# A hand-made scheduler's step estimates are set to the durations of a trace (windowed attention and two MLPs, one core)

## The chip, the core and the metric

One core of a Trainium2 chip runs the whole program as one launch. TensorE (PE) multiplies, VectorE (DVE) and ScalarE (ACT) do everything elementwise, GpSimd (POOL) only sets up constants, and SyncE (SP) issues all transfers. The metric is the device time of a launch in microseconds (us), compared as medians.

## What is computed

The reference, cut to what matters (`q`, `k`, `v` are 4 x 8 x 576 x 64, so 2304 tokens of width 512; both MLPs are 512 to 2048 to 512, all in float32):

```
scores = scale * q @ k.T;  scores = where(0 <= rel < 64, scores, -1e9)     # causal window of 64
attn   = exp(scores - max);  attn = attn / (sum(attn) + 1e-9)
x      = (attn @ v), heads side by side                                     # 2304 x 512
h = x @ w_in;  x = relu(h)**2 @ w_out                                       # first MLP
h = x @ w_in;  P = a0 + a1*h + a2*h*h + a3*h*h*h                            # second MLP, with its own weights
Q = 1 + |b0|*|h| + |b1|*h*h;  out = (P / (Q + 1e-6)) @ w_out
```

## The kernel before, in words

**Arithmetic.** Each float32 matrix of an MLP is split into a high and a low part (`wih`, `wil`, `wo`, `xh`, `xl`, `g` for both parts), and a product is three matmuls: high by high, high by low, low by high. So a weight tile that comes from memory first goes through `convert` (lines 355 to 394): a load into one of three `raw` buffers, an ACT operation (L369), three DVE operations on the bits (L371, L374, L377), a rounding on ACT (L388: the high part) and a subtraction on DVE (L389: the low part).

**Tiles and stages.** Tokens go in five blocks (four of 512, one of 256), the hidden width in 16 steps `j` of 128. Layer 0 (the first MLP) works through the blocks; a step is 12 matmuls `h` (L552, into PSUM buffers `h0`, `h1`), `mid1` on ACT and DVE (L618 relu, L620 and L623 or L624 squares, L625 the low part of `g`), and 12 matmuls into the accumulators `acc0` to `acc3` (L571), one step later. While block 0 runs, its weights are converted, and while each block runs, the attention of the next is done in between: per 128 tokens transposes of `q` and `k` (L435, L448), scores (L470), softmax on DVE, ACT and DVE (`top` L485, `exp` L490, `norm` L494 to L496), transposes of the probabilities (L507) and their product with `v` (L523), with copies out of PSUM in between (L440, L456 or L457, L512, L535, L536). The first block's attention stands alone at the start. Layer 1's weights are converted during blocks 1 to 3, stored to memory and loaded again. Layer 1 (the second MLP) has the same loops with `mid2` (L664 to L686: three ACT reads of `h`, then seven DVE operations, a logarithm and an exponential on ACT, and a rounding L685), its outputs two steps behind `h`; `h` has four PSUM buffers there. `evac2` copies the accumulators out and stores them.

**What sets the order.** Nothing is written in its final order. Each step is added to a `Plan` with its possible engines and for each an estimate in nanoseconds, its reads and writes, and sometimes a due time. `Plan.run` (L90) then builds a timetable by the estimates: it always takes the item and engine that can start first (the engine free, the inputs ready and a gap of 150 to 200 passed, 2000 after a load), and among equal starts the one that is due first. A step with two engines (copies, roundings, one of the squares) goes to the one on which it starts first. The items are emitted in that order, so the estimates decide the order of rows in each engine's queue and which of two engines does a step. They decide nothing else: at run time each engine works strictly through its own queue, waiting for semaphores. SP's loads are items too, with their own estimates.

```
119    key = (start, it.due)
295    MM = {n: 0.4167 * n + 3 for n in (256, 512)}        # one matmul of the MLPs
498    plan.add({"dve": 850}, top, [ps], [t, nm])
499    plan.add({"act": 1550}, exp, [nm, t], [t, su])
```

`act(n, psum, ptr)` and `dve(n, fast, ptr)` (L133, L137) are the estimates of an elementwise operation on n columns: `psum` when it reads PSUM, `fast` for the double rate, `ptr` for operands that are one value per partition. `start` and `span` (L297 to L305), from which the due times of both MLPs follow, are made of `MM`.

## Time and profile before

| | us |
|---|---|
| median of three runs | 895.03 |
| lowest | 893.75 |
| the profiled execution, on the device | 894.46 |
| its span in the trace (first to last instruction) | 892.7 |
| TensorE busy (matmuls) | 877.6 |
| VectorE busy | 667.3 |
| ScalarE busy | 570.2 |

Times in the trace are from the span's start. An engine's busy time counts overlapping instructions once, and ends of matmuls are modelled, so a busy TensorE need not be at its peak. In the rows further down, a bracket behind an instruction gives the idle time of its engine just before it and what ended it.

### The profile page before, as it was taken

How to read it: one execution, taken by the hardware profiler on the slowest of the kernel's cores; microseconds unless marked ns; L12 is line 12 of the kernel's file. 1: busy time of each engine (PE TensorE's matmuls, PEld its weight loads, DVE VectorE, ACT ScalarE, POOL GpSimd, SP SyncE). 2: the span in 40 equal slices, each digit the busy share in tenths (PEclk: the TensorE clock that was granted, in tenths of full speed). 3: DMA queues.
4: the chain of work that ended last, by engine and by line, in shares of the span. 5: the costliest groups of instructions: out<-in, count | busy, mean ns of one | idle time of the engine just before them, and what ended most of it. 6: DMA issues, size and time to landing. Idle time of an engine off the chain costs nothing.

```text
span 892.7 us, 14126 instructions
## 1 busy us (share of the span) xinstructions
PE 877.6 (98%) x5200; PEld 730.2 (82%) x5200; DVE 667.3 (75%) x1428; ACT 570.2 (64%) x1187; POOL 3.1 (0%) x17
## 2 busy tenths in 40 slices
PE   7899999999999999999999999999999999999998
PEld 6677788888878888888899888888888888988886
DVE  6999999878587842422131799999999999999994
ACT  6886777667566653443344766676667666888764
POOL 1000000000000000000000000000000000000000
PEclk9999999999999999999999999999999999999999
DMA  9796676878878721200079920210011002100001
GB/s 219 199 242 180 194 215 209 268 234 262 257 246 246 239 64 37 94 1 1 1 284 370 355 76 1 67 75 1 1 48 47 1 1 95 48 1 24 1 0 48
DMA packets 133573, 110.50 MB, mean 124 GB/s; under 512 B 79488, under 2 KB 112256, under 8 KB 131456
## 3 DMA queue, kind: packets, MB, share of 16 engines
q1 hardware_dynamic: 133504, 109.60, 39.1%
q8 instruction: 41, 0.67, 0.3%
q14 instruction: 28, 0.23, 0.1%
HBM read 78.65 MB, written 30.93 MB: 123 GB/s over the span
## 4 chain that ended last, share of the span: by engine, by line
PE 86%; DVE 8%; DMA 3%; ACT 2%; issue 1%; SPq 0%; POOL 0%; POOLq 0%; ACTq 0%; DVEq 0%
PE h L552 29%; PE acc L573 22%; PE acc L571 18%; PE t L552 11%; DMA raw<-in_moe_w_out_dram 2%; PE t L523 2%; DVE cvr L374 1%; DMA raw<-in_moe_w_in_dram 1%; PE t L470 1%; DVE cvr L377 1%; PE t L507 1%; DVE raw L371 1%; PE t L448 1%; DVE sm L485 1%; PE t L435 0%
## 5 line engine op out<-in xcount | busy, mean ns | idle before, releaser
L571 PE MATMUL acc<-g,wo 128*128 128x512 f32 (+1 forms) x960 | 216.0, 372 | 0.2 <-DVE g L625 0.2
L571 PEld LDWEIGHTS acc<-g,wo 128*128 128x128 f32 x960 | 166.4, 189 | 31.1 <-issue 0.9
L552 PE MATMUL h<-xh,wih 128*128 128x512 f32 (+1 forms) x480 | 181.9, 379 | 1.1 <-ACT xh L535 0.6
L552 PE MATMUL h<-xh,wil 128*128 128x512 f32 (+1 forms) x480 | 177.4, 370 | 1.1 <-DVE wil L389 1.1
L552 PE MATMUL h<-xl,wih 128*128 128x512 f32 (+1 forms) x480 | 177.3, 369 | 0.3 <-DVE xl L536 0.3
L625 DVE TENSOR_TENSOR g<-cvr,g 128x512 fp32r<-128x512 f32 (+1 forms) x80 | 50.8, 635 | 103.3 <-ACT cvr L623 103.0
L618 ACT ACTIVATE cvr<-h 128x512 f32<-128x512 f32 (+1 forms) x80 | 44.2, 553 | 95.7 <-PE h L552 90.5
L552 PEld LDWEIGHTS h<-xh,wil 128*128 128x128 f32 x480 | 90.5, 189 | 18.0 <-DVE wil L389 2.4
L552 PEld LDWEIGHTS h<-xh,wih 128*128 128x128 f32 x480 | 90.5, 189 | 17.7 <-issue 1.4
L552 PEld LDWEIGHTS h<-xl,wih 128*128 128x128 f32 x480 | 90.6, 189 | 14.2 <-DVE xl L536 0.7
L573 PE MATMUL acc<-wo,cvr 128*128 128x512 f32 x384 | 93.1, 390 | 0.0
L573 PE MATMUL acc<-wo,g 128*128 128x512 f32 x384 | 93.1, 390 | 0.0
L573 PEld LDWEIGHTS acc<-wo,g 128*128 128x128 f32 x384 | 71.6, 188 | 14.5
L573 PEld LDWEIGHTS acc<-wo,cvr 128*128 128x128 f32 x384 | 71.5, 188 | 14.4
L669 DVE SCALAR_TENSOR_TENSOR kT<-kT,b,sm 128x512 f32<-128x512 f32 (+1 forms) x80 | 55.7, 696 | 16.4 <-ACT kT L664 13.6
L671 ACT ACTIVATE raw<-kT,cb 128x512 f32<-128x512 f32 (+1 forms) x80 | 54.9, 686 | 8.7 <-DVE kT L669 4.6
L552 PE MATMUL t<-xl,wih 128*128 128x512 f32 (+1 forms) x160 | 58.9, 368 | 0.0
L552 PE MATMUL t<-xh,wil 128*128 128x512 f32 (+1 forms) x160 | 58.8, 368 | 0.0
L552 PE MATMUL t<-xh,wih 128*128 128x512 f32 (+1 forms) x160 | 58.8, 368 | 0.0
L369 ACT ACTIVATE cvr<-raw 128x512 f32<-128x512 f32 x64 | 42.7, 671 | 24.2 <-DMA raw<-in_moe_w_out_dram 14.5
L682 DVE SCALAR_TENSOR_TENSOR pT<-pT,coef,raw 128x512 f32<-128x512 f32 (+1 forms) x80 | 55.6, 695 | 1.7
L673 ACT ACTIVATE raw<-raw,cb 128x512 f32<-128x512 f32 (+1 forms) x80 | 54.5, 681 | 1.8
(143 smaller groups left out, 1332.1 us busy)
## 6 DMA issues: line engine op xcount, KB each, us to landing
raw<-in_moe_w_in_dram SPq DMA_DIRECT2D x64, 256.0 KB, 3.8
raw<-in_moe_w_out_dram SPq DMA_DIRECT2D x32, 512.0 KB, 4.2
w2h_d<-raw SPq DMA_DIRECT2D x32, 256.0 KB, 2.8
w2l_d<-cvr SPq DMA_DIRECT2D x32, 256.0 KB, 3.1
ld<-in_v_dram SPq DMA_DIRECT2D x25, 256.0 KB, 3.8
out_dram<-ld SPq DMA_DIRECT2D x18, 256.0 KB, 2.0
x2h_d<-xh SPq DMA_DIRECT2D x4, 1024.0 KB, 4.4
x2l_d<-xl SPq DMA_DIRECT2D x4, 1024.0 KB, 5.7
```

Source lines behind the costliest of these rows:

```text
L369: plan.add({"act": act(DM)}, lambda e: A.activation(out=t.t, in_=raw.t.bitcast(F32)[:, :, 1], func=ACTF.Copy, scale=2.0 ** -112), [raw], [t])
L371: plan.add({"dve": dve(DM, True)}, lambda e: V.tensor_scalar(out=raw.t[:, :, 1], in0=raw.t[:, :, 1], scalar1=0x80000000, scalar2=None, op0 ...
L523: T.matmul(out=ps.t[e * 64:(e + 1) * 64, hp, gl * W:(gl + 1) * W], lhsT=vg[gl].t[:, 2 * hp + e, :], rhs=pt[gl].t[:, hp, (e ^ gl) * 64:((e ...
L552: T.matmul(out=v4(hp.t, n), lhsT=w.t[:, (c ^ 2) * 128:((c ^ 2) + 1) * 128], rhs=x.t[:, :n // 128, c, :], start=(c == 0 and z == 0), stop=( ...
L571: T.matmul(out=v4(acc[l, bi, m].t, n), lhsT=w.t[:, m, :], rhs=y.t[:, :n // 128, :], start=st, stop=en)
L573: T.matmul(out=v4(acc[l, bi, m].t, DM), lhsT=y.t[:, m, :], rhs=w.t, start=st, stop=en)
L618: plan.add({"act": act(n, True)}, lambda e: A.activation(out=r.t[:, :n], in_=hp.t[:, :n], func=ACTF.Relu), [hp], [r])
L625: plan.add({"dve": dve(n)}, lambda e: V.tensor_tensor(out=gl.t[:, :nq], in0=v4(r.t, n), in1=gh.t[:, :nq].bitcast(F32), op=ALU.subtract), [ ...
L669: plan.add({"dve": dve(n, ptr=1)}, lambda e: V.scalar_tensor_tensor(out=f(h2), in0=f(h2), scalar=b1, in1=f(ab), op0=ALU.mult, op1=ALU.add) ...
L671: plan.add({"act": act(n, ptr=1)}, lambda e: A.activation(out=f(y), in_=f(h2), func=ACTF.Ln, scale=2.0 ** -63, bias=cb[:, 0:1]), [h2], [y])
L673: plan.add({"act": act(n, ptr=1)}, lambda e: A.activation(out=f(y), in_=f(y), func=ACTF.Exp, scale=-1.0, bias=cb[:, 1:2]), [y], [y])
L682: plan.add({"dve": dve(n, ptr=1)}, lambda e: V.scalar_tensor_tensor(out=f(u), in0=f(u), scalar=coef[:, 0:1], in1=f(y), op0=ALU.subtract, o ...
```

## The change

Only numbers that `Plan` reads are changed; no operation, buffer, load or loop is touched.

```diff
 def act(n, psum=False, ptr=0):
-    return (50 if psum else 92) + 0.836 * n + 93 * ptr
+    return (150 if psum else 180) + 0.86 * n + 90 * ptr
...
 def dve(n, fast=False, ptr=0):
-    return 68 + 1.042 * n / (2 if fast else 1) + 61 * ptr
+    return 160 + 1.03 * n / (2 if fast else 1) + 63 * ptr
...
-    MM = {n: 0.4167 * n + 3 for n in (256, 512)}
+    MM = {n: 0.4167 * n + 13.6 for n in (256, 512)}
...
-        plan.add({"dve": 850}, top, [ps], [t, nm])
-        plan.add({"act": 1550}, exp, [nm, t], [t, su])
+        plan.add({"dve": 1470}, top, [ps], [t, nm])
+        plan.add({"act": 2310}, exp, [nm, t], [t, su])
```

Besides: transposes 430 to 450, the scores 900 to 1250, the product with `v` 1250 to 1280. `norm` stays at 1050, the loads keep theirs. For 512 columns `act` goes from 478 to 590 (PSUM) and from 520 to 620 (SBUF), `dve` from 602 to 687, a matmul from 216.4 to 227.0.

What stands elsewhere now, at three places. In the names, the number behind an underscore counts buffers and differs between the two programs.

**First place: ScalarE's queue at the start**, the attention of block 0. `wih11`, `wil11`, `wih10`, `wil10` here are buffers in which softmax of the first and second 128 tokens works (`nm` and `su` its maxima and sums); `qT` and `kT` are transposed inputs. Before:

```order
L456 COPY kT0_209<-t0_204 128x4x128
L440 COPY qT0_221<-h0_214 128x512
L456 COPY kT1_219<-t1_243 128x4x128
L490 ACTIVATE wih11_248,su0_268<-wih11_248,nm0_249 128x128 x4
L490 ACTIVATE wil11_262,su1_302<-wil11_262,nm1_263 128x128 x4
L440 COPY qT0_319<-acc3_314 128x512
L512 COPY wo5_351<-t1_328 128x512
L490 ACTIVATE wih10_353,su2_376<-wih10_353,nm2_354 128x128 x4
```

After:

```order
L456 COPY kT0_209<-t0_204 128x4x128
L440 COPY qT0_221<-h0_214 128x512
L456 COPY kT1_219<-t1_245 128x4x128
L440 COPY qT1_264<-h1_256 128x512
L490 ACTIVATE wih11_250,su0_277<-wih11_250,nm0_251 128x128 x4
L490 ACTIVATE wil11_266,su1_313<-wil11_266,nm1_267 128x128 x4
L490 ACTIVATE wih10_318,su2_339<-wih10_318,nm2_319 128x128 x4
L440 COPY qT0_366<-acc3_304 128x512
```

The copy of `qT1` is new in this queue (before, VectorE did it behind eight pieces of L485), and the copy of the third `qT` has moved behind a third group of exponentials.

**Second place: one step of the second MLP in its steady state**, block 1. First TensorE, where the `h` of one step ends and the outputs (L573) of the step two before follow. Before:

```order
L552 MATMUL h1_6309<-xl0_5389,wih10_5142 128x512
L552 MATMUL h1_6309<-xh0_5363,wil10_5149 128x512
L573 MATMUL acc0_5985<-wo4_1371,g_719 128x512 x3
L573 MATMUL acc1_5992<-wo4_1371,g_719 128x512 x3
L573 MATMUL acc2_6001<-wo4_1371,g_719 128x512 x3
L573 MATMUL acc3_6006<-wo4_1371,g_719 128x512 x3
L552 MATMUL t1_6351<-xh0_5363,wih11_5174 128x512
```

After:

```order
L552 MATMUL h1_6284<-xl0_5347,wih10_5107 128x512
L552 MATMUL h1_6284<-xh0_5322,wil10_5115 128x512
L552 MATMUL t1_6326<-xh0_5322,wih11_5142 128x512
L552 MATMUL t1_6326<-xl0_5347,wih11_5142 128x512
L552 MATMUL t1_6326<-xh0_5322,wil11_5150 128x512
L573 MATMUL acc0_5984<-wo4_1361,g_735 128x512 x3
L573 MATMUL acc1_5991<-wo4_1361,g_735 128x512 x3
```

Three matmuls of the next step's `h` now stand ahead of the outputs. On VectorE, around the same step; `pT1` is the numerator `u` of a step, `kT` its denominator, `raw` the reciprocal. Before:

```order
L682 SCALAR_TENSOR_TENSOR pT1_6297<-pT1_6297,coef_182,raw2_6307 128x512
L685 CAST g_719<-pT1_6297 128x4x128
L669 SCALAR_TENSOR_TENSOR kT0_6336<-kT0_6336,b1_184,sm0_6330 128x512
L686 TENSOR_TENSOR g_719<-pT1_6297,g_719 128x4x128
L675 TENSOR_TENSOR pT0_6339<-pT0_6339,h1_6309 128x512
L676 SCALAR_TENSOR_TENSOR pT0_6339<-pT0_6339,coef_182,h1_6309 128x512
```

After:

```order
L669 SCALAR_TENSOR_TENSOR kT0_6336<-kT0_6336,b1_184,sm0_6330 128x512
L682 SCALAR_TENSOR_TENSOR pT1_6299<-pT1_6299,coef_182,raw2_6306 128x512
L675 TENSOR_TENSOR pT0_6341<-pT0_6341,h1_6284 128x512
L676 SCALAR_TENSOR_TENSOR pT0_6341<-pT0_6341,coef_182,h1_6284 128x512
L686 TENSOR_TENSOR g_735<-pT1_6299,g_735 128x4x128
```

L682 of a step stands behind L669 of the next, its rounding (L685) has gone to ScalarE, and L686 follows two rows of the next step later.

**Third place: VectorE's last rows.** `kT0_8457` before and `kT0_8451` after belong to the last step but one, whose first row L669 is; `xl0` takes the low parts of older steps. Before:

```order
L682 SCALAR_TENSOR_TENSOR pT1_8409<-pT1_8409,coef_182,raw0_8419 128x512
L686 TENSOR_TENSOR xl0_6556<-pT1_8409,xh0_6542 128x4x128
L669 SCALAR_TENSOR_TENSOR kT0_8457<-kT0_8457,b1_184,sm0_8451 128x512
L675 TENSOR_TENSOR pT0_8462<-pT0_8462,h1_8421 128x512
L676 SCALAR_TENSOR_TENSOR pT0_8462<-pT0_8462,coef_182,h1_8421 128x512
```

After:

```order
L682 SCALAR_TENSOR_TENSOR pT0_8428<-pT0_8428,coef_182,raw2_8405 128x512
L669 SCALAR_TENSOR_TENSOR kT0_8451<-kT0_8451,b1_184,sm0_8445 128x512
L682 SCALAR_TENSOR_TENSOR pT1_8433<-pT1_8433,coef_182,raw0_8422 128x512
L686 TENSOR_TENSOR xl0_6556<-pT0_8428,xh0_6542 128x4x128
L669 SCALAR_TENSOR_TENSOR kT1_8467<-kT1_8467,b1_184,sm1_8457 128x512
L686 TENSOR_TENSOR xl0_6556<-pT1_8433,xh0_6542 128x4x128
```

One L682 and two L686 of older steps now stand behind the first L669 of the last two steps.

## Rows read from the trace of the kernel before

**Rows 1.** The page's busy times: us, share of the span, instructions.

```profile
PE 877.6 (98%) x5200; PEld 730.2 (82%) x5200; DVE 667.3 (75%) x1428; ACT 570.2 (64%) x1187; POOL 3.1 (0%) x17
```

**Rows 2.** Stretches: their length, each engine's busy us, TensorE's granted clock, DMA share, GB/s.

```profile
0.00:20.00 20.00, 14.90 (x191) 12.98 (x192) 11.57 (x64) 12.74 (x48) 3.14 (x17) 1.00 0.94 216
20.00:40.00 20.00, 15.88 (x207) 12.48 (x206) 18.16 (x64) 16.01 (x52) 0.00 (x0) 0.91 0.71 193
40.00:80.00 40.00, 39.34 (x290) 31.09 (x289) 38.95 (x103) 33.22 (x83) 0.00 (x0) 1.00 0.80 219
80.00:120.00 40.00, 39.16 (x235) 31.14 (x234) 37.74 (x94) 30.07 (x70) 0.00 (x0) 1.00 0.66 191
...
500.00:740.00 240.00, 240.00 (x1060) 198.79 (x1059) 223.07 (x345) 158.65 (x251) 0.00 (x0) 1.00 0.14 49
```

**Rows 3.** Timeline of VectorE and ScalarE at three places: start us, us, instruction.

```profile
9.09 0.28 DVE L485 CUSTOM_DVE_ANT_0 wih<-acc,mask 128x128 f32<-128x128 f32 x1
...
9.30 0.29 DVE L485 CUSTOM_DVE_ANT_0 wih<-acc,mask 128x128 f32<-128x128 f32 x1
...
9.82 0.41 ACT L490 ACTIVATE wih<-wih,nm 128x128 f32<-128x128 f32 x1
...
10.21 0.39 ACT L490 ACTIVATE wih<-wih,nm 128x128 f32<-128x128 f32 x1
...
861.18 0.69 DVE L675 TENSOR_TENSOR pT<-pT,h 128x512 f32<-128x512 f32 x1
861.79 0.68 DVE L686 TENSOR_TENSOR xl<-pT,xh 128x512 fp32r<-128x512 f32 x1
...
865.33 0.59 ACT L664 ACTIVATE kT<-t 128x512 f32<-128x512 f32 x1
865.81 0.78 ACT L667 ACTIVATE pT<-t,na 128x512 f32<-128x512 f32 x1
```

**Rows 4.** Timeline of the start: second scores, the first two steps of `h`.

```profile
11.40 0.33 PE L470 MATMUL t<-kT,qT 64*64 64x128 f32 x2 [1.23 <-DVE qT L440]
...
33.75 0.51 PE L552 MATMUL h<-xh,wih 128*128 128x512 f32 x1 [0.55 <-ACT xh L535]
...
39.53 0.50 PE L552 MATMUL h<-xh,wil 128*128 128x512 f32 x1 [0.84 <-DVE wil L389]
```

**Rows 5.** Timeline: low halves of weight tiles 9 and 12, and the matmuls that use them.

```profile
92.90 0.68 DVE L389 TENSOR_TENSOR wil<-cvr,wih 128x512 fp32r<-128x512 f32 x1
...
95.48 0.39 PE L552 MATMUL h<-xh,wil 128*128 128x512 f32 x1
...
111.76 0.68 DVE L389 TENSOR_TENSOR wil<-cvr,wih 128x512 fp32r<-128x512 f32 x1
...
116.21 0.40 PE L552 MATMUL h<-xh,wil 128*128 128x512 f32 x1
```

**Rows 6.** Timeline around 257 us: exponentials, normalisation, transpose.

```profile
254.46 0.19 ACT L490 ACTIVATION_READ_ACCUMULATOR sm<-sm,nm 128x1 f32 x1
...
255.76 0.16 DVE L494 TENSOR_SCALAR rs<-su 128x4 f32<-128x4 f32 x1
...
257.00 0.63 PE L507 MATMUL t<-ident,sm 128*128 128x128 f32 x4 [0.84 <-DVE sm L496]
```

**Rows 7.** Timeline of the second MLP's steady state, one step.

```profile
639.89 2.88 PE L573 MATMUL acc<-wo,g 128*128 128x512 f32 x12
...
645.33 2.88 PE L573 MATMUL acc<-wo,cvr 128*128 128x512 f32 x12
...
641.29 0.75 DVE L669 SCALAR_TENSOR_TENSOR kT<-kT,b,sm 128x512 f32<-128x512 f32 x1
641.96 0.68 DVE L686 TENSOR_TENSOR cvr<-pT,cvr 128x512 fp32r<-128x512 f32 x1
```

**Rows 8.** Timeline of the end: the last two parts of `g`, the last matmuls.

```profile
880.90 1.46 DVE L686 TENSOR_TENSOR cvr<-pT,cvr 128x512 fp32r<-128x512 f32 x2
...
883.59 5.60 PE L573 MATMUL acc<-wo,cvr 128*128 128x512 f32 x24
```

More of the change, by code (lines that the diff above doesn't have):

```diff
@@ L435, in tr @@
                 T.transpose(ps.t[:, c, :], s[:, c * 128:(c + 1) * 128], ident)
-        plan.add({"pe": 430}, tr, [src], [ps], due)
+        plan.add({"pe": 450}, tr, [src], [ps], due)
         t = qT[i] = buf(QTP, [128, HP, 128])
@@ L448, in tr @@
                 T.transpose(ps.t[:, c, :], s[:, c * 128:(c + 1) * 128], ident)
-        plan.add({"pe": 430}, tr, [src], [ps], due)
+        plan.add({"pe": 450}, tr, [src], [ps], due)
         t = kT[i] = buf(KTP, [128, HP, W + 128])
@@ L471, in mm @@
                                  rhs=kt.t[r, hp, gl * W:gl * W + 128], start=True, stop=True)
-        plan.add({"pe": 900}, mm, [qt, kt], ps, due)
+        plan.add({"pe": 1250}, mm, [qt, kt], ps, due)
         for gl in range(2):
@@ L507, in tr @@
                 T.transpose(ps.t[:, c, :], src.t[:, c, :], ident)
-        plan.add({"pe": 430}, tr, [src], [ps], due)
+        plan.add({"pe": 450}, tr, [src], [ps], due)
         t = pT[i, n] = early(NF - 5 - i, 2 + n, 128) if i < NS0 else buf(PT, [128, 4, 128])
@@ L528, in mm @@
                         )
-        plan.add({"pe": 1250}, mm, vg + pt, [ps], due)
+        plan.add({"pe": 1280}, mm, vg + pt, [ps], due)
         bi, o = sub_block[i]
```

## The prediction

> **What bounds the kernel now.** First the page's busy times: TensorE is busy 877.6 of 892.7 us, so all its idle time together is 15.1 us [rows 1]. Then the table of stretches: 5.1 us of that lie in the first 20 us, 4.1 in the next 20, 0.7 in 40 to 80, 0.8 in 80 to 120, and in 500 to 740 there is none [rows 2]; one piece of 0.8 lies at 257 [rows 6], and the rest at the end and in pieces too short to matter. The program's matmuls are the same before and after, 5200 of them [rows 1], so removed waits can give at most 15.1 us, and that only with no start and no end. The second thing to read there is VectorE: 39.0 of 40 us in 40 to 80 and 37.7 in 80 to 120. In that stretch it converts the weights of the first MLP and does the attention of the second block, and TensorE runs just behind it: the idle pieces are waits of `h` for a weight tile (0.84 us at 39.5 [rows 4]). From 120 us on only TensorE matters, and an order of ACT and VectorE can cost there but hardly gain.
>
> **What the new numbers are against the trace.** The old ACT and DVE numbers are the distances at which instructions follow each other, the new ones the durations, and these two differ. On VectorE 128x512 operations last 0.69 and 0.68 and start 0.61 apart; on ScalarE a read of PSUM lasts 0.59 and the next starts 0.48 after it [rows 3]. The old formulas say 602 and 478, the new ones 687 and 590. The four row maxima of a softmax are the worst: pieces of 0.28 start 0.21 apart, 0.84 us for four, where the old number is 850 and the new one 1470; the exponentials follow at 0.39, 1.56 us for four, where 1550 becomes 2310 [rows 3]. On TensorE it is the other way: the 24 512-wide matmuls of a step (twelve outputs, twelve `h`) take 639.89 to 645.33, 226.7 ns each [rows 7], the new formula gives 227.0, the old one 216.4. So the planner now knows TensorE better and takes ScalarE and VectorE to be 15% slower, and a softmax 40% slower (4830 in all instead of 3450), than they are.
>
> The Trainium skill ("Perfetto Trace Analysis", Optimizing Scalar/DVE Operations) says that profiled latency holds a write acknowledgement that overlaps with the next instruction, so it is more than the engine's occupation; rows 3 agree. Its page "VectorE: DVE Perf Modes" (The DRAIN you can't avoid) says that the next operation starts only when the pipe has emptied, which would make the durations the occupation and the new numbers the true ones; rows 3 speak against it here.
>
> What such errors do: a planner that takes an engine for slower than it is puts the consumers on TensorE later, which gives slack, but it sorts the rows of ScalarE and VectorE by readiness times that are not the real ones, and those queues run strictly in order. It also evens out the two engines: of the last rounding of `g` (L685) ScalarE gets 74 rows instead of 50, of the square (L623) 60 instead of 67. No instruction is added or removed, and the loads are the same ones; SP issues them in a slightly other order, the first weight tile's ahead of two loads of `v` that are needed 10 us later.
>
> **Term 1, the start and the first block (0 to 120 us): -0.5.** The copy of `qT1` moves from VectorE, where scores 1 waited for it (idle to 11.40 [rows 4]), to ScalarE ahead of the exponentials, so scores 1 can start about 1 us sooner. In exchange the copy of `qT0` stands behind three groups of exponentials instead of two: scores 2 comes up to 1.56 us later. Stepping on through both new queues with the distances of rows 3, ScalarE is then never idle to the eighth group, the first `h` starts at about 32.3 instead of 33.75 and the low half of the second weight tile is there at 37.6 instead of 39.5 [rows 4]: between 1.3 and 1.9 us gained, g below. It can also be nothing: the granted clock of 0.91 in 20 to 40 [rows 2] means 3.6 us at the lower level of 1.2 GHz, after a stretch in which TensorE was often idle, so 1.8 us of matmul time hang on where such a piece falls, and I stepped at full clock. The gain isn't kept either, because VectorE sets the pace next. Counting VectorE's rows ahead of the low half of a weight tile, each with its distance (0.61 [rows 3], 0.67 with a pointer operand [rows 7], 0.21 for a piece of L485 [rows 3], and so on for the shorter forms), its work there goes from 80.4 to 83.2 us for tile 9 and from 99.2 to 103.5 for tile 12 (the two largest increases of the sixteen; for tile 10 it falls by 0.3), while TensorE's work ahead of the matmuls that need them grows by 0.4 and 0.9. The slack in the trace is 95.48 - 93.58 = 1.9 us at tile 9 and 116.21 - 112.44 = 3.8 at tile 12 [rows 5]. So tile 9 makes TensorE 2.8 - 0.4 - 1.9 - g = 0.5 - g later, tile 12 4.3 - 0.9 - 3.8 - g = -0.4 - g: with g of 1.9 a gain of 1.4 survives, with g of 0 a loss of 0.5 comes. I take -0.5, nearer the middle, since stepping through up to tile 8 left about that. The unknown on the other side: loads into the three `raw` buffers. VectorE's idle time in 40 to 120 is 1.05 + 2.26 = 3.3 us [rows 2]; if the new order holds raw tiles so long that this doubles, the term is +3.3.
>
> **Term 2, the boundary of the third block (257 us): -0.4.** A transpose of probabilities waits 0.84 us. The exponentials it needs ended at 254.65, but VectorE came to the normalisation at 255.76 only [rows 6], behind five other rows since the row maxima. Three stand there now, which lets it come 1.1 us sooner, when the exponentials end. The transpose itself stands three matmuls (0.7 us) earlier in the new order and then waits 0.84 - 1.1 + 0.7 = 0.4; -0.4, bounds -0.84 and 0.
>
> **Term 3, the second MLP (500 to 870 us): 0.** TensorE's output matmuls of a step move behind three matmuls of the next `h` (second place in the section on the change), 0.68 us later. VectorE's rows: `u` of a step (L682) now stands behind L669 of the next step, and three instead of two rows lie between it and L686, as the cast is on ScalarE. From 641.29, where L669 of the next step starts, 1.40 us after the end of its `h` [rows 7], the new chain is 0.67 + 0.67 + 0.61 + 0.67 + 0.68 = 3.3 us: L686 ends 4.7 us after that `h`. The outputs start 5.44 + 0.68 = 6.1 us after it, so 1.4 us of slack are left where the trace has 645.33 - 642.64 = 2.7 [rows 7]. No wait; if the chain were 1.4 us longer there would be one in each of 64 steps.
>
> **Term 4, the end: +0.4.** Behind the last L669 pair VectorE used to have only the last two steps; in the new order it still has three older rows (L682, L686, L686), 1.87 us, and gets to the first of these L669 1.3 us later, of which its idle time before takes about 1.4. The last `g` was ready at 882.36 and its partner at 881.58, for matmuls that start at 883.59, where the low part is first read by the third matmul, at 884.04 [rows 8]. So the partner comes at 883.4 to 884.7, and the wait is 0 to 0.7; the last outputs and stores keep their places. I take +0.4, bounds 0 and 1.3 (1.3, if that idle time can't be used).
>
> The sum against the profiled execution's own 894.46 us (span 892.7): -0.5 - 0.4 + 0 + 0.4 = -0.5, so **894.0 us**. The two runs of 893.75 and 895.03 lie around that execution; the median of the three shown is 0.6 above it. By bounds: 894.46 - 1.4 - 0.8 = 892.3 and 894.46 + 3.3 + 1.3 = 899.1.
>
> **The rivals.**
> - *The new numbers are truer where it counts.* If a duration were the time for which an engine is taken, the old plan was too tight, and the waits inside it (0.66 and 0.84 us in 40 to 120 [rows 2], 0.84 at 257 [rows 6]) go as planned waits would. 894.46 - 2.3 = 892.1 us. (This is what the rule of the DRAIN, named above from the Trainium skill, would make of it.) For it: PE's number is truer. Against: rows 3. Chance 0.15.
> - *The change does nothing that can be seen.* The terms cancel within the spread of runs; 894.5. Against: nearly every row of the queues moved. I count it with the forecast.
> - *VectorE falls behind in the first block.* It is 97% busy there [rows 2], and in the new order it gets more of the squares (20 of 80 instead of 13). Raw tiles are freed later, loads land later; +3.3 and the end's +1.3 make 899.1. Chance 0.15.
> - *The second MLP stalls at each step (slower by over 2%).* The place is L682 behind L669 and the cast on ScalarE behind the logarithm of the next step; the point is 1.4 us of slack. Were the chain 1.8 us longer than I add up, each of 64 steps would wait 0.4 us if TensorE can't catch up, 26 us: 920 us. For it: a late step delays the next `h` buffer too. Against: VectorE has 17 idle us in 500 to 740 [rows 2], and slack doesn't add up over steps. Chance 0.05.
>
> **How the numbers follow.** The forecast has 0.64 with its own range 892.3 to 897; 0.15 each for 892.1 and 899.1, 0.05 for 920, 0.01 for a gain over 2%, which would be 17.9 us where all idle time is 15.1. The range from 891.0 to 899.5 leaves out the last two and the edges of the others, under 2 in 10. By the 2% that a measurement of this kernel can tell from no change (17.9 us): faster 0.01, within 0.94, slower 0.05.
>
> **What would show it.** Term 1: the first `h` near 32.3 and its second weight tile near 37.6, but the matmuls around 90 us at most 1.5 us earlier than before; wrong if TensorE's idle time in 40 to 120 passes 3 us (1.5 now). Term 2: no wait of a transpose for `sm` near 256. Term 3: TensorE 240 of 240 us busy in 500 to 740, the outputs 6.1 us after the `h`. Term 4: a wait of 0 to 0.7 us ahead of the last 24 matmuls. The forecast is wrong above all if TensorE shows repeated short waits for `g` in the second MLP.

## The result, and the profile after

The changed kernel takes 902.63 us (901.27 to 903.55, four runs), the kernel before 894.47: a ratio of 1.0094, 95% interval [1.0078, 1.0110]; one of the four runs of the kernel before took 2247.93 us and is no part of the ratio. That is 8 us slower, within 2%, and outside the range of the forecast (891.0 to 899.5). The profiled execution took 903.07, its span is 901.3 where it was 892.7.

The busy times, then stretches of 40 and 240 us of the changed kernel (columns as in [rows 2]: length, busy us of TensorE, its weight loads, VectorE, ScalarE, GpSimd, granted clock, DMA share, GB/s):

```profile
PE 881.1 (98%) x5200; PEld 730.7 (81%) x5200; DVE 656.5 (73%) x1413; ACT 571.4 (63%) x1202; POOL 3.1 (0%) x17
```

```profile
40.00:80.00 40.00, 36.88 (x243) 28.77 (x242) 35.42 (x82) 28.63 (x69) 0.00 (x0) 0.96 0.62 191
80.00:120.00 40.00, 37.89 (x251) 29.77 (x250) 36.70 (x97) 28.76 (x73) 0.00 (x0) 1.00 0.60 177
...
500.00:740.00 240.00, 240.00 (x1077) 199.35 (x1075) 205.34 (x319) 166.96 (x270) 0.00 (x0) 1.00 0.18 62
```

Beside [rows 2], TensorE's idle time in 40 to 120 grows from 1.5 to 3.12 + 2.11 = 5.2 us, and VectorE's, the engine that sets the pace there, from 3.3 to 4.58 + 3.30 = 7.9. From 500 to 740 TensorE has no idle time, as before. So most of the loss lies where the first block runs and converts weights. Three matmuls that stand at the same place of the program show it: the first `h`, the first of the ninth step and the first of the third block's ninth (the 1st, 97th and 481st matmul of L552). Before, the first of them is in [rows 4], at 33.75, the others here:

```profile
87.98 0.50 PE L552 MATMUL h<-xh,wih 128*128 128x512 f32 x1 [0.44 <-ACT wih L388]
...
300.31 0.39 PE L552 MATMUL h<-xh,wih 128*128 128x512 f32 x1
```

After:

```profile
33.66 0.50 PE L552 MATMUL h<-xh,wih 128*128 128x512 f32 x1
...
92.19 0.50 PE L552 MATMUL h<-xh,wih 128*128 128x512 f32 x1 [0.29 <-ACT wih L388]
...
308.56 0.39 PE L552 MATMUL h<-xh,wih 128*128 128x512 f32 x1
```

0.1 us early at the first, 4.2 late at the second, 8.3 late at the third, and 8.6 at the end of the span.

What a loss looks like: TensorE, VectorE, ScalarE and the load issue of the changed kernel from 40 to 52 us. Brackets give the idle time before an instruction and what ended it.

```profile
39.98 0.46 SPq L316 DMA_DIRECT2D raw<-in_moe_w_in_dram  x1
...
44.75 0.67 ACT L369 ACTIVATE cvr<-raw 128x512 f32<-128x512 f32 x1 [2.02 <-DMA raw<-in_moe_w_in_dram]
...
45.33 0.58 ACT L618 ACTIVATE cvr<-h 128x512 f32<-128x512 f32 x1
45.45 0.43 DVE L371 TENSOR_SCALAR raw<-raw 128x512 uint32<-128x512 uint32 x1 [0.55 <-ACT cvr L369]
...
46.31 0.63 ACT L620 ACTIVATE g<-cvr 128x512 fp32r<-128x512 f32 x1
...
46.99 0.50 PE L571 MATMUL acc<-g,wo 128*128 128x512 f32 x1 [1.31 <-ACT g L620]
...
48.14 0.69 DVE L625 TENSOR_TENSOR g<-cvr,g 128x512 fp32r<-128x512 f32 x1
...
48.88 1.60 PE L571 MATMUL acc<-g,wo 128*128 128x512 f32 x5 [1.39 <-DVE g L625]
...
50.27 0.63 PE L552 MATMUL h<-xh,wih 128*128 128x512 f32 x1
...
50.70 0.63 PE L552 MATMUL h<-xl,wih 128*128 128x512 f32 x1
```

ScalarE reaches L369 while its weight tile is still on the way (issued at 39.98, landed at 44.65) and waits 2.02 us. Behind L369 in its queue stand the relu of the step (L618), a rounding and L620; VectorE waits for the same tile (0.55), and TensorE twice for `g` (1.31 and 1.39). Then it runs at its lower level of 1.2 GHz: from 50.27 on seven matmuls start 0.43 apart instead of 0.23, 1.4 us. Before, the load of this tile was issued no sooner (its two pieces at 40.10 and 40.52, here at 39.55 and 39.98) and landed at 43.97, but the relu, both squares and the reader of another tile stood ahead of its reader, and the tile was there when ScalarE came to it (ScalarE alone, the relu and this reader):

```profile
42.43 0.58 ACT L618 ACTIVATE cvr<-h 128x512 f32<-128x512 f32 x1
...
44.98 0.73 ACT L369 ACTIVATE cvr<-raw 128x512 f32<-128x512 f32 x1
```

So the load isn't issued later, and lands only 0.7 us later; but ScalarE comes to its reader 2.3 us sooner (42.73, then it waits), and behind it waits even the reader of a tile that had landed at 42.38.

This repeats. ScalarE's waits for loads in the first 130 us (us in total, times, longest), first before, then after:

```profile
ACT cvr L369 <- DMA raw<-in_moe_w_in_dram: 3.7, 3, 2.3
...
ACT cvr L369 <- DMA raw<-in_moe_w_out_dram: 2.5, 4, 1.1
```

```profile
ACT cvr L369 <- DMA raw<-in_moe_w_out_dram: 9.2, 8, 2.0
ACT cvr L369 <- DMA raw<-in_moe_w_in_dram: 6.7, 6, 2.0
```

And the largest of VectorE's waits after, 40 to 130 us; it was 2.7 us in four times before:

```profile
DVE raw L371 <- ACT cvr L369: 5.9, 8, 1.3
```

What TensorE itself waits for there, 5.8 us in all, is put down to VectorE's L625 (1.8 us), to ScalarE's L620 and copies L512 (1.3 and 1.2), to a load of `q` (0.7) and to smaller ones; it isn't VectorE alone.

**Where the 8.6 us of the span are.** In 40 to 130 TensorE is busy 84.19 of 90 us, 88.50 before: 4.3. In 130 to 300 its idle time is 1.78 instead of 0.84: 0.9. The lower clock after the wait at 48.88: 1.4. The end: 0.4. The start: -0.1. Each wait also hides some 0.17 us, since a matmul's row lasts 0.39 or 0.40 while the next could start 0.23 after it; with some six waits more that is 1.0. Together 7.9; the rest isn't placed.

### The profile page after: what moved, and what is told of

It reads as the page before. It is cut to its first block, busy times and chain, and to the rows that moved or that the text cites. A ratio compares the mean times of both kernels' runs of the same rounds, so it can differ in the third digit from the quotient of the medians.

```text
span 901.3 us, 14146 instructions
## 1 busy us (share of the span) xinstructions
PE 881.1 (98%) x5200; PEld 730.7 (81%) x5200; DVE 656.5 (73%) x1413; ACT 571.4 (63%) x1202; POOL 3.1 (0%) x17
## 4 chain that ended last, share of the span: by engine, by line
PE 86%; DMA 5%; DVE 4%; SPq 2%; ACT 2%; issue 1%; ACTq 0%; DVEq 0%
PE h L552 30%; PE acc L573 22%; PE acc L571 18%; PE t L552 11%; SPq L316 2%; PE t L523 2%; DMA raw<-in_moe_w_in_dram 1%; PE t L470 1%; DMA raw<-in_moe_w_out_dram 1%; DMA ld<-in_q_dram 1%; PE t L507 1%; DMA w2h_d<-raw 1%; DVE cvr L374 1%; DVE cvr L377 1%; DVE raw L371 1%
## 5 line engine op out<-in xcount | busy, mean ns | idle before, releaser
L571 PE MATMUL acc<-g,wo 128*128 128x512 f32 (+1 forms) x960 | 216.4, 372 | 3.1 <-DVE g L625 1.8
L552 PE MATMUL h<-xh,wih 128*128 128x512 f32 (+1 forms) x480 | 182.9, 381 | 0.5 <-ACT wih L388 0.3
L552 PE MATMUL h<-xh,wil 128*128 128x512 f32 (+1 forms) x480 | 178.2, 371 | 1.0 <-DVE wil L389 0.9
L552 PE MATMUL h<-xl,wih 128*128 128x512 f32 (+1 forms) x480 | 177.8, 370 | 0.0
L625 DVE TENSOR_TENSOR g<-cvr,g 128x512 fp32r<-128x512 f32 (+1 forms) x80 | 50.8, 635 | 96.4 <-ACT cvr L623 96.2
L552 PEld LDWEIGHTS h<-xh,wil 128*128 128x128 f32 x480 | 90.8, 189 | 19.1 <-DVE wil L389 3.5
L552 PEld LDWEIGHTS h<-xh,wih 128*128 128x128 f32 x480 | 90.8, 189 | 17.2 <-ACT wih L388 1.4
L552 PEld LDWEIGHTS h<-xl,wih 128*128 128x128 f32 x480 | 91.1, 190 | 14.0
L618 ACT ACTIVATE cvr<-h 128x512 f32<-128x512 f32 (+1 forms) x80 | 44.2, 553 | 90.1 <-PE h L552 87.0
L573 PE MATMUL acc<-wo,cvr 128*128 128x512 f32 x384 | 93.3, 390 | 0.0
L573 PE MATMUL acc<-wo,g 128*128 128x512 f32 x384 | 93.1, 389 | 0.0
L573 PEld LDWEIGHTS acc<-wo,cvr 128*128 128x128 f32 x384 | 71.5, 188 | 15.1 <-DVE cvr L686 0.4
L573 PEld LDWEIGHTS acc<-wo,g 128*128 128x128 f32 x384 | 71.6, 188 | 14.6
L669 DVE SCALAR_TENSOR_TENSOR kT<-kT,b,sm 128x512 f32<-128x512 f32 (+1 forms) x80 | 55.7, 696 | 25.8 <-ACT kT L664 25.5
L369 ACT ACTIVATE cvr<-raw 128x512 f32<-128x512 f32 x64 | 42.7, 670 | 45.6 <-DMA raw<-in_moe_w_out_dram 27.6
L552 PE MATMUL t<-xl,wih 128*128 128x512 f32 (+1 forms) x160 | 58.9, 368 | 0.0
L552 PE MATMUL t<-xh,wil 128*128 128x512 f32 (+1 forms) x160 | 58.8, 368 | 0.0
L552 PE MATMUL t<-xh,wih 128*128 128x512 f32 (+1 forms) x160 | 58.8, 368 | 0.0
L682 DVE SCALAR_TENSOR_TENSOR pT<-pT,coef,raw 128x512 f32<-128x512 f32 (+1 forms) x80 | 55.4, 694 | 0.0
```

Source lines behind the costliest of these rows:

```text
L369: plan.add({"act": act(DM)}, lambda e: A.activation(out=t.t, in_=raw.t.bitcast(F32)[:, :, 1], func=ACTF.Copy, scale=2.0 ** -112), [raw], [t])
L552: T.matmul(out=v4(hp.t, n), lhsT=w.t[:, (c ^ 2) * 128:((c ^ 2) + 1) * 128], rhs=x.t[:, :n // 128, c, :], start=(c == 0 and z == 0), stop=( ...
L571: T.matmul(out=v4(acc[l, bi, m].t, n), lhsT=w.t[:, m, :], rhs=y.t[:, :n // 128, :], start=st, stop=en)
L573: T.matmul(out=v4(acc[l, bi, m].t, DM), lhsT=y.t[:, m, :], rhs=w.t, start=st, stop=en)
L618: plan.add({"act": act(n, True)}, lambda e: A.activation(out=r.t[:, :n], in_=hp.t[:, :n], func=ACTF.Relu), [hp], [r])
L625: plan.add({"dve": dve(n)}, lambda e: V.tensor_tensor(out=gl.t[:, :nq], in0=v4(r.t, n), in1=gh.t[:, :nq].bitcast(F32), op=ALU.subtract), [ ...
```

## The experiments

All change numbers that the plan reads, as the change does; e8 alone moves rows by a rule. Old and new stand for the numbers before and after; "load" is what the plan counts from the start of a weight tile's load to its reader (1456 ns and a lead of 2000). "VectorE idle" is 90 us less its busy time in the stretch from 40 to 130, "L369" what ScalarE waited there for loads from 20 to 130. Medians; ratios to the kernel before on the same chip, and a cost "by the ratio" is that share of 894.5 us. The last two columns are of the one profiled execution, which in e1 (902.9), e7 (894.8) and e18 (899.1) lay at the edge of its kernel's runs.

| run | ScalarE, VectorE | softmax | TensorE | load | us | ratio, 95% | VectorE idle | L369 |
|---|---|---|---|---|---|---|---|---|
| before | old | old | old | 3.46 | 894.5 | | 3.6 | 6.2 |
| after | new | new | new | 3.46 | 902.6 | 1.0094 [1.0078, 1.0110] | 9.1 | 15.9 |
| e1 | old | old | new | 3.46 | 906.4 | 1.0133 [1.0102, 1.0165] | 5.4 | 11.8 |
| e2 | new | new | old | 3.46 | 903.7 | 1.0105 [1.0085, 1.0125] | 10.7 | 14.3 |
| e3 | old | new | old | 3.46 | 901.6 | 1.0085 [1.0064, 1.0106] | 7.4 | 13.2 |
| e4 | new | new | new | 4.06 | 899.2 | 1.0056 [1.0024, 1.0088] | 8.0 | 11.3 |
| e5 | all by chance +-3%, seed 1 | | | | 896.7 | 1.0021 [1.0006, 1.0036] | 4.6 | 7.2 |
| e6 | the same, seed 2 | | | | 896.3 | 1.0020 [1.0005, 1.0036] | 5.0 | 8.5 |
| e7 | old | old | old | 2.86 | 897.9 | 1.0032 [1.0015, 1.0048] | 4.2 | 10.8 |
| e8 | after, L369 two rows later | | | | 904.1 | 1.0114 [1.0077, 1.0151] | 12.2 | 2.8 |
| e9 | old x1.15 | x1.15 | old | 3.46 | 904.2 | 1.0105 [1.0077, 1.0132] | 11.5 | 11.9 |
| e10 | old x0.90 | x0.90 | old | 3.46 | 906.8 | 1.0139 [1.0107, 1.0171] | 2.1 | 6.4 |
| e11 | old | old | new | 4.06 | 895.7 | 1.0010 [0.9995, 1.0025] | 4.6 | 10.3 |
| e12 | old | old | old | 3.89 | 894.6 | 0.9995 [0.9981, 1.0009] | 4.9 | 2.3 |
| e13 | new | new | new | 4.66 | 898.6 | 1.0045 [1.0027, 1.0063] | 8.4 | 12.6 |
| e14 | new | old | new | 4.06 | 895.6 | 1.0017 [1.0004, 1.0031] | 6.5 | 6.9 |
| e15 | old | new | new | 4.06 | 897.3 | 1.0023 [1.0009, 1.0036] | 4.6 | 6.9 |
| e16 | old x1.15 | x1.15 | old | 4.06 | 899.6 | 1.0054 [1.0038, 1.0070] | 8.1 | 10.5 |
| e17 | old | old | matmul new | 3.46 | 899.6 | 1.0050 [1.0033, 1.0067] | 4.5 | 4.9 |
| e18 | old | old | all but matmul new | 3.46 | 895.3 | 1.0013 [0.9999, 1.0026] | 4.7 | 4.3 |

### Which of the numbers (e1 to e4)

e1 has the first of these new lines, e2 the second and third, e3 the third alone. e4 is the change and the last line.

```diff
+    MM = {n: 0.4167 * n + 13.6 for n in (256, 512)}      # e1, with 450, 1250, 1280
+    return (150 if psum else 180) + 0.86 * n + 90 * ptr  # e2: act, and dve likewise
+        plan.add({"dve": 1470}, top, [ps], [t, nm])       # e2, e3, and exp 2310
-            return 2000
+            return 2600                                   # e4
```

> Only TensorE's numbers are new (matmul +10.6 ns, transposes 450, scores 1250, product with v 1280); ScalarE and VectorE keep the old ones. Before 894.5, after 902.6. Theory A (the loads): in the new plan everything on ScalarE and VectorE is 15 to 40% longer while a load keeps its 1456 + 2000 ns, so fewer rows stand between a load and the L369 that reads it, and at run time ScalarE waits for the load with the relu behind it (15.9 us at L369 in the first 130 us after, 6.2 before). With the old numbers there: no change, 893 to 896, L369 waits at most 8 us. Theory B (the overload): the new plan takes VectorE for overfull, so TensorE waits in the plan itself and the order keeps those waits; here VectorE gets more room, 893 to 895. Theory C (TensorE's numbers, by the due times made of them, move the order for the worse): 900 or more.

> Only ScalarE's and VectorE's numbers are new (both formulas, row maxima 1470, exponentials 2310); TensorE's are the old ones. A and B: all of the loss is here, 901 to 906; with the shorter TensorE steps somewhat worse than after rather than better, since the plan then takes TensorE for faster still against the other two. C: 893 to 896.

> Only the two softmax numbers are new (850 to 1470, 1550 to 2310). The first block holds eight softmaxes of the next one: 8 x 0.62 = 5.0 us more on VectorE and 8 x 0.76 = 6.1 on ScalarE in the plan; the 15% on all other rows there is some 13 us on VectorE (of about 90). If the loss goes with the work added in the plan (A and B alike): about a quarter of it, 896 to 897. If it hangs on the softmax being the one that is most wrong (40%): 900 or more. C: no change.

> The changed kernel, and in addition the plan's lead from a load to its reader is 2600 ns instead of 2000, so a load of a weight tile counts 4.06 us instead of 3.46, longer by the same 17% as the rows of the other engines. A: L369's waits for loads in the first 130 us fall from 15.9 to 8 us or less and the time to 895 to 897. B: those waits fall too, but TensorE is late all the same, 900 to 904. C: 901 to 904.

Each part alone costs about as much as the whole or more: by the ratio 12, 9 and 8 us against 8. So the parts aren't terms of a sum, and none of A, B and C fits all four: e1 came as C said and falsified the expectation that TensorE's truer numbers do no harm, e2 as A and B said, e3 as it should if the softmax is what costs. e1 loses elsewhere: VectorE's idle time is moderate (5.4), TensorE's grows more in 130 to 300 (4.5 us, 0.8 before) than in 40 to 130 (4.1, 1.5 before), and it waits for its own loads of `q`, which before it did not (e1, 40 to 300 us):

```profile
PE t L435 <- DMA ld<-in_q_dram: 2.9, 2, 1.6
```

e4 gives back 3.4 of 8 us, less than theory A wanted (895 to 897) and more than B (900 to 904): a plan with short loads is a part of the cause, not all. Its six runs spread from 895.7 to 904.4 and the two intervals overlap; e13 below, with still longer loads, is clear of the change.

### Is any other order worse? (e5, e6)

```diff
+        engines = {e: t * self.rng.uniform(1 - 0.03, 1 + 0.03) for e, t in engines.items()}
```

> The kernel before, each single estimate of the plan multiplied by a random factor between 0.97 and 1.03 (seed 1): errors without a direction. TensorE's numbers alone, ScalarE's and VectorE's alone and the softmax numbers alone each cost 7 to 12 us, which does not add up to the 8 us of all together. Theory F (the old order is a lucky one, found by trying numbers; any other order loses): 900 to 906. Theory A (errors with a direction cost: rows taken for longer against the loads): within 893 to 897.

> As the one with seed 1, with seed 2. F: 900 to 906, and the two seeds differ by some us. A: within 893 to 897.

1.9 and 1.8 us by the ratio, inside what A gave and far from F's 900. The old order isn't a lucky one: errors without a direction move rows about everywhere and cost a quarter of the change. That it is the direction that costs, and not the size, isn't shown: these errors are at most 3%, those of the change 5% on a matmul, about 15% on most rows and 40% on a softmax, and chance errors of that size weren't run. For the direction speaks e17 below, where 5% on the matmul alone costs 4.5 us.

### Shorter loads, and the reader moved by hand (e7, e8)

```diff
-            return 2000
+            return 1400                                   # e7
...
+            while m < len(order) and passed < 2 and it not in order[m].deps:   # e8, for each L369
+                passed += order[m].on == it.on and not order[m].late
+                m += 1
+            order.insert(m - 1, order.pop(n))
```

> The kernel before, and the plan's lead from a load to its reader is 1400 ns instead of 2000: a weight tile counts 2.86 us instead of 3.46, 17% less, all rows as before. If A holds (it is the ratio of loads to rows that counts), this does the same as the change: L369's waits for loads in 20 to 130 us rise from 6 to 14 or more, 899 to 905. If the loads play no part: 893 to 896.

> The changed kernel, and once the order stands, each L369 (the first reader of a loaded weight tile) is moved behind the next two ScalarE rows that may go ahead of it. If the loss comes from the relu and the squares that stand behind a waiting L369: its waits for loads shrink to under 8 us in 20 to 130 and 2 to 5 us of the 8 come back, 897 to 900. If the weight tile itself is what TensorE waits for in the end: the waits shrink and the time stays or rises, 901 to 906.

e7 misses A's 899 to 905 and the 893 to 896 of the other side: loads taken for 17% too short, by themselves, cost 2.9 us by the ratio. e8 tests what the picture at 44.75 suggested: putting the relu ahead of the waiting L369 is not enough. ScalarE's waits for loads nearly vanish (15.9 to 2.8), and the kernel is no faster, rather slower (904.1; the intervals overlap), because VectorE now waits for the tile instead (line numbers of that kernel are 9 higher, L380 is L371 and L378 is L369):

```profile
DVE raw L380 <- ACT cvr L378: 10.5, 12, 2.3
```

VectorE's idle time, 12.2 us, is the largest of all runs, and half of TensorE's 8.3 us in 40 to 130 is then a wait for VectorE's low part of `g` (L634 is L625):

```profile
PE acc L580 <- DVE g L634: 4.2, 3, 2.4
```

### The size and the sign of the error (e9, e10, e16)

```diff
+    return 1.15 * ((50 if psum else 92) + 0.836 * n + 93 * ptr)   # e9, e16; 0.9 in e10
+    return 1.15 * (68 + 1.042 * n / (2 if fast else 1) + 61 * ptr)
+        plan.add({"dve": 978}, top, [ps], [t, nm])                # exp 1782, norm 1208
+            return 2600                                           # e16 only
```

> The kernel before, all its estimates of ScalarE and VectorE times 1.15, the softmax's too (978, 1782, 1208); TensorE and loads as before. Theory A2: VectorE sets the pace from 40 to 130 us, and what costs there is its idle time (3.6 us before, 9.1 after); a plan that takes both elementwise engines for slower than they are against TensorE and the loads puts rows at the head of VectorE's queue whose input is not there yet. Then 15% without the extra error of the softmax already costs: VectorE idle 6 us or more in 40 to 130, 898 to 903. Theory S: what costs is the softmax alone, taken for 40% too long against the other rows (softmax numbers alone: 901.6); then 894 to 897 here.

> As e9_scale115, but times 0.90 (softmax 765, 1395, 945). A2 in its one-sided form (only rows that are planned too long hurt): VectorE idle at most 4 us in 40 to 130, 893 to 896. Two-sided form (any error with a direction puts rows in the wrong order): 897 or more, and then the waits should show up as TensorE's, for rows that ScalarE and VectorE deliver later than planned, in the second MLP too.

> e9_scale115 (all ScalarE and VectorE numbers times 1.15: 904.2) with the lead from a load to its reader at 2600 ns, so a weight tile counts 4.06 us, 17% more too; TensorE as before. If the ratio to the loads is what costs: 895 to 897, VectorE idle 4 to 5 us in 40 to 130 (11.5 in e9). If the ratio to TensorE does: 900 to 904. In between, 897 to 900, each has its share.

All ScalarE and VectorE numbers 15% too long, with nothing else touched, make the whole loss and a little more (e9): VectorE's idle time goes from 3.6 to 11.5. That is theory A2, with 904.2 somewhat beyond its 898 to 903; the softmax's extra error isn't needed. The stretch from 40 to 130 in e9, and two of VectorE's waits there; for TensorE (second line) it didn't wait in the changed kernel:

```profile
40.00:130.00 90.00, 82.92 (x532) 64.62 (x530) 78.52 (x191) 64.88 (x153) 0.00 (x0) 0.98 0.62 182
```

```profile
DVE raw L371 <- ACT cvr L369: 4.3, 6, 1.1
DVE xh L535 <- PE t L523: 2.4, 2, 1.3
```

10% too short is no better (e10, 906.8), the two-sided form. There VectorE is busier from 40 to 130 than in any other run (idle 2.1 us), and TensorE is late all the same; 2.1 us of it in the second MLP, where outputs wait for `g` and for an accumulator's copy (TensorE's waits from 500 to 860, a stretch in which it waits in no other run):

```profile
PE acc L573 <- DVE cvr L685: 0.8, 1, 0.8
PE acc L573 <- ACT ld L695: 0.8, 1, 0.8
PE acc L573 <- DVE cvr L686: 0.5, 2, 0.3
```

e16 makes the loads 17% longer as well and gets half of e9's loss back (899.6, in between as the expectation has it; VectorE idle 8.1, not 4 to 5). That agrees with the two kinds of waits in e9: elementwise rows that are too long cost once against the loads and once against TensorE.

### Longer loads with the other numbers (e11 to e15)

```diff
+            return 2600          # e11, with TensorE's new numbers; e14, e15
+            return 2300          # e12, and size / 330 instead of size / 360
+            return 3200          # e13, on the changed kernel
```

> TensorE's new numbers alone (906.4) with the lead from a load to its reader at 2600 ns instead of 2000. Those numbers are the truer ones of TensorE, and still they cost 12 us, where the trace shows transposes that wait for loads of q (L435, 2.9 us in two places, and 2.2 in one with no named cause at 259) and ScalarE at L369 for weight tiles (14.7 us in 20 to 130, 6.4 before). Theory P: the old, too short matmul was a margin that hid the load's too short estimate; with the load longer the truer numbers lose nothing: 893 to 897. If the due times that are made of the matmul's number are to blame, this changes little: 902 to 907.

> The kernel before with loads taken for longer: lead 2300 instead of 2000 and 330 instead of 360 bytes per ns, so a weight tile counts 3.89 us instead of 3.46. The other way round from e7 (2.86 us: 897.9). If waiting for loads is what is left to gain: L369's waits below 4 us in 20 to 130 and 892 to 894; if the old numbers were already at the flat bottom: 893.5 to 896.

> The changed kernel with the lead from a load to its reader at 3200 ns (2000 in the change, 2600 in e4_after_gap26: 899.2). If the loads alone are to blame and 2600 was only half way: 895 to 897. If what is left are the elementwise rows, 15 to 40% too long against TensorE: 898 to 901.

> e4_after_gap26 with the old softmax numbers (850, 1550); both formulas stay new. If the softmax's numbers make what is left of the loss (899.2 against 895.7 of e11_pe_gap26, which has all elementwise numbers old): 895 to 897. If the formulas do: 898 to 900.

> e4_after_gap26 with the old formulas for ScalarE and VectorE; the softmax's numbers stay new. The counterpart of e14_after_gap26_oldsoft: 898 to 900 if the softmax's numbers make what is left, 895 to 897 if the formulas do; both at 897 to 898 if each makes half.

e11 is the clearest of the study (the 14.7 us in its expectation are L369's waits for VectorE and for loads together; for loads alone they are 11.8): the same TensorE numbers that cost 12 us cost 0.9 once the plan takes a weight tile's load for 4.06 us (by the ratio; zero lies in the interval). The loads of the trace agree: the longest in the changed kernel's chain of waits from 40 to 130 (start, us, what) last

```profile
39.98 4.67 DMA raw<-in_moe_w_in_dram
...
98.69 4.65 DMA raw<-in_moe_w_in_dram
...
120.19 3.84 DMA raw<-in_moe_w_in_dram
```

where the plan has 3.46. They didn't get slower by the change: the longest in the chain of the kernel before last 4.16, 4.52 and 4.76. With the old numbers everywhere, longer loads gain nothing (e12), though ScalarE's waits for them fall to 2.3 us; with the old numbers those waits cost nothing. e13 shows that still longer loads don't cure the change either (898.6): what is left are the elementwise numbers. Of these, with the longer lead, the formulas alone leave a loss of 1.5 us by the ratio (e14) and the softmax's two numbers alone one of 2.1 (e15), the two together 5.0 (e4, whose interval goes from 2.1 to 7.9). So e14 came as it should if the softmax's numbers make what is left, and e15 as if each makes half; the intervals don't decide it. In e14 the formulas are 15% too long and the loads 17% longer, about one ratio, which may be why so little is lost.

### Which of TensorE's numbers (e17, e18)

```diff
+    MM = {n: 0.4167 * n + 13.6 for n in (256, 512)}      # e17; e18: 450, 1250, 1280 only
```

> The kernel before with only the MLPs' matmul at the measured 227.0 ns (216.4 before). If the matmul's number, and with it the due times, is what cost in e1_pe: 902 or more. If the others are: 894 to 897.

> The counterpart of e17_mm: transposes 450, scores 1250, product with v 1280, matmul as before. If these cost in e1_pe: 902 or more; if the matmul does: 894 to 897. Both at 897 to 900 if each takes a part.

The matmul's number costs 4.5 us by the ratio, between the two expectations, the others 1.2 (zero lies in the interval); both together cost 12. Here the parts plainly don't add up. Why the pair does so much isn't settled; that longer loads cure it is (e11). A fourth `raw` buffer, which might take the wait for a load away instead of moving it, wasn't tried.

No version of the eighteen is faster than the kernel before; e11, e12 and e18 can't be told from it.

## Why the prediction was wrong, step by step

**What bounds the kernel** held: TensorE at its end, VectorE setting the pace in the first block, an order that can cost there and hardly gain.

**What the new numbers are** held, with one addition (last section). That ScalarE and VectorE were set 15% too long, and that this sorts queues by times that aren't real, is what e9 shows to be enough for the whole loss. I had the mechanism and took it for harmless in size. "PE's number is truer" was right as a reading and wrong as an argument for the change: truer alone, it costs 12 us (e1).

**Term 1 is the step that failed**: -0.5 forecast, about +7 measured. The start went partly as stepped through (TensorE after, beside [rows 4]):

```profile
10.34 0.33 PE L470 MATMUL t<-kT,qT 64*64 64x128 f32 x2 [0.29 <-ACT qT L440]
...
38.98 0.50 PE L552 MATMUL h<-xh,wil 128*128 128x512 f32 x1 [0.63 <-DVE wil L389]
```

Scores 1 came at 10.34 instead of 11.40, but the first `h` at 33.66, not 32.3, and the second weight tile's matmul at 38.98, not 37.6, so the gain g was 0.1 to 0.6 instead of 1.3 to 1.9. The stepping missed a wait: in TensorE's new order a transpose of `q` (L435) stands ahead of transposes of probabilities that went before it, and its load isn't there yet; the first of those, whose input was ready at 23.18, starts 2.1 us after that, which is more than the missing gain.

```profile
24.82 0.63 PE L435 MATMUL h<-ident,ld 128*128 128x128 f32 x4 [2.65 <-DMA ld<-in_q_dram]
25.28 0.60 PE L507 MATMUL acc<-ident,wih 128*128 128x128 f32 x4
```

Then the sum compared VectorE's own work ahead of two weight tiles with the slack in [rows 5]. That work it counted nearly right. Here are the stretches up to the low halves of tiles 9 and 12 (columns as above, the third busy time is VectorE's), before and after:

```profile
0.00:92.90 92.90, 82.35 (x739) 66.08 (x740) 79.97 (x257) 70.94 (x203) 3.14 (x17) 0.98 0.79 208
0.00:111.76 111.76, 101.04 (x877) 80.87 (x878) 98.83 (x305) 86.25 (x240) 3.14 (x17) 0.98 0.77 207
```

```profile
0.00:99.10 99.10, 86.59 (x753) 69.30 (x754) 83.30 (x260) 72.29 (x203) 3.14 (x17) 0.97 0.72 195
0.00:121.80 121.80, 107.47 (x899) 85.54 (x900) 103.82 (x313) 87.72 (x241) 3.14 (x17) 0.97 0.70 194
```

VectorE's work grew by 3.3 us (2.8 forecast) and 5.0 (4.3). What the sum put at nothing is its idle time, the rest of each stretch: 12.9 us ahead of either tile before, 15.8 and 18.0 after. At tile 10, where the work grew by 0.2 (90.44 and 90.62), the low half comes 4.5 later (103.37 and 107.82), nearly all of it idle time. TensorE's idle time in 40 to 120 is 5.2, beyond the 3 us that the prediction named as its own sign of being wrong. The unknown was named, loads that land late, and bounded by a doubling of VectorE's 3.3 us (+3.3); it grew to 7.9, and the waits brought a piece that wasn't in the bound, the lower clock behind two of them (1.4 us). So the rival "VectorE falls behind in the first block" came nearest, priced 3.5 us too low and given 0.15. Its stated reason, more squares on VectorE, is a part at most, as tile 10 shows, and its way from there, raw tiles freed later and loads later, isn't what the place at 44.75 shows: there the load was issued no later, and its reader came 2.3 us sooner.

**Term 2** failed with it: -0.4 forecast, +0.7 measured. The transpose waits 1.53 us where it was 0.84 [rows 6]. Three rows of VectorE lie between the row maxima and the normalisation, as forecast, and it starts 0.3 us after the exponentials (1.1 before); but the exponentials themselves stand behind another L369 that waits for its load (ScalarE and TensorE around 260 us):

```profile
259.43 0.67 ACT L369 ACTIVATE cvr<-raw 128x512 f32<-128x512 f32 x1 [3.15 <-DMA raw<-in_moe_w_out_dram]
...
260.94 0.41 ACT L490 ACTIVATE sm<-sm,nm 128x128 f32<-128x128 f32 x1
...
264.14 0.63 PE L507 MATMUL t<-ident,sm 128*128 128x128 f32 x4 [1.53 <-DVE sm L496]
```

**Term 3** held to a tenth (one step after, beside [rows 7]):

```profile
647.97 0.39 PE L552 MATMUL t<-xh,wil 128*128 128x512 f32 x1
...
649.61 0.75 DVE L669 SCALAR_TENSOR_TENSOR kT<-kT,b,sm 128x512 f32<-128x512 f32 x1 [0.71 <-ACT kT L664]
...
652.32 0.69 DVE L686 TENSOR_TENSOR cvr<-pT,cvr 128x512 fp32r<-128x512 f32 x1
...
654.32 1.07 PE L573 MATMUL acc<-wo,cvr 128*128 128x512 f32 x4
```

The `h` ends at 648.20, L669 starts 1.41 after it (1.40), L686 ends 4.81 after it (4.7), the outputs start 6.12 after it (6.1), so 1.3 us of slack are left (1.4). TensorE is busy 240 of 240 us in 500 to 740.

**Term 4** held: +0.4. The last L686 pair starts at 891.79, and the last 24 matmuls take 5.96 us instead of 5.60 [rows 8]:

```profile
891.79 1.35 DVE L686 TENSOR_TENSOR cvr<-pT,cvr 128x512 fp32r<-128x512 f32 x2
891.86 5.96 PE L573 MATMUL acc<-wo,cvr 128*128 128x512 f32 x24
```

**The other rivals.** "The new numbers are truer where it counts" is out by e2 and e9, "nothing that can be seen" by the interval. The stall at each step of the second MLP didn't come; e10, 10% the other way, has four waits in its 64 steps, 2.1 us.

**What is shown and what isn't.** Shown: a 15% error of the elementwise numbers alone makes the loss (e9), chance errors of up to 3% make a quarter of it (e5, e6); in the changed kernel most of it lies in the first block, where VectorE idles for 9.1 us instead of 3.6, and moving the waiting ScalarE row gains nothing (e8); longer loads in the plan give a part back (e4, e13, e16) and nearly all where TensorE's numbers alone are new (e11). Not shown: that VectorE's idle time there sets the loss in every version. e1 and e10 lose 12 us with 5.4 and 2.1 us of it, e14 loses 1.5 with 6.5. Nor that the direction of the errors costs and not their size. Not settled: how the parts combine, TensorE's (e1, e17, e18) above all.

## What to carry to other kernels

As far as these runs go, a planner's table works by its ratios: setting some entries nearer to the trace while loads stay too short, or while others are durations and not distances, can cost more than leaving all of them a little wrong; change them together, take an engine's entry from the distance at which its instructions follow each other, and look what the plan adds to it before a reader. When the engine that sets the pace works in order, ask of a new order how long that engine will stand idle, not how much work lies ahead of a row. Random errors of a few per cent are a cheap test of whether an order is robust before its numbers are tuned.

## What the runs showed of the hardware that I had not expected

The distance of two VectorE operations depends on whether the second reads what the first wrote. In the changed kernel:

```profile
645.50 0.68 DVE L675 TENSOR_TENSOR pT<-pT,h 128x512 f32<-128x512 f32 x1
...
646.22 0.75 DVE L676 SCALAR_TENSOR_TENSOR pT<-pT,coef,h 128x512 f32<-128x512 f32 x1
...
646.88 0.69 DVE L686 TENSOR_TENSOR g<-pT,g 128x512 fp32r<-128x512 f32 x1
...
647.48 0.68 DVE L678 SCALAR_TENSOR_TENSOR kT<-kT,raw 128x512 f32<-128x512 f32 x1
...
648.20 0.69 DVE L680 SCALAR_TENSOR_TENSOR raw<-kT,raw 128x512 f32<-128x512 f32 x1
```

L676 reads the `pT` that L675 wrote and starts 0.72 us after it, L680 reads the `kT` of L678 and does the same; L678 has nothing to do with L686 and starts 0.60 after it, before L686's 0.69 are over. So a dependent neighbour costs a little more than the duration, an independent one the old formula's 0.60. The Trainium skill ("VectorE: DVE Perf Modes", The DRAIN you can't avoid) has the next operation start when the pipe has emptied, and adds that one that is not held starts earlier; the prediction gave the first half alone. By these rows the dependent one does wait (0.72) and the independent one doesn't (0.60).

The old numbers had both cases, because the plan adds its gap of 150 ns before every reader. For 512 columns on VectorE 602 + 150 = 752 ns stand against the 0.72 here and against the 0.74 from L625 at 48.14 to the matmul that waited for it at 48.88; on ScalarE 520 + 150 = 670 against the 0.68 from L620 at 46.31 to the matmul at 46.99. The new numbers make 837 and 770 of them: about 0.1 us too long for a reader too, since the plan's gap already holds the end of the duration.

TensorE's lower level of 1.2 GHz came behind the two waits that ended at 46.99 and 48.88, and lasted from 50.27 to 53.26: these 2.7 us of waiting cost 1.4 more. Not all waiting does: in e3 TensorE is idle for 7.1 us in 40 to 130, for 5.8 in the changed kernel, and its granted clock there is 1.00.
